# Attention and two expert layers on one core: copies, masks and minus maxima written by ScalarE, maxima over two PSUM banks, a predicated mean of v

## The chip, the cores and the metric

The kernel runs on one core of a Trainium2 chip. The metric is the device time of one execution in microseconds (us). Before the change three runs took 762.19, 762.69 and 763.52 us; the median is 762.69 us.

## The reference

For 2 batches of 8 heads, 768 rows and 64 columns a clustered attention is computed; its output goes through a dense layer and then through a layer of 8 experts. The change touches only the attention:

```python
q_assign = np.argmax(np.einsum('bhsd,hcd->bhsc', q_n, c_n), axis=-1)   # 16 clusters
k_assign = np.argmax(np.einsum('bhsd,hcd->bhsc', k_n, c_n), axis=-1)
mask = q_assign[:, :, :, None] == k_assign[:, :, None, :]
scores = scale * np.matmul(q, k.transpose(0, 1, 3, 2))
scores = np.where(mask, scores, -1000000000.0)
scores = scores - np.max(scores, axis=-1, keepdims=True)
attn = np.exp(scores)
attn = attn / (np.sum(attn, axis=-1, keepdims=True) + 1e-09)
return np.matmul(attn, v)
```

A row of q whose cluster holds no key has only masked scores, all alike, so its output is the mean of v.

## The kernel before, in words

A head has 6 blocks of 128 rows of q and of k (`NC` = 6) and is worked on in two halves of 3 blocks (`HC` = 3), called units. 16 heads make 32 units, 16 for each batch. The numbers are fp32, held as an f16 part and an f16 remainder, so that TensorE works in f16.

- `load` brings k, q and v of a head by DMA; `prep1` writes the f16 parts and remainders of k and q into `pk1` (a ScalarE copy, a GpSimd subtraction) and sends `pk1` through a transposing DMA on SP's queue into `tk1` (head 0: through TensorE).
- `prep2` finds the clusters. TensorE multiplies with the centroids (`sim`), VectorE makes the one-hot matrix `oh` (maximum, comparison, tie-break with the weights `wt_c`). It then builds `pk2`, four blocks of 6 x 128 columns: 64 columns of q or k parts, 16 columns of one-hot mask times 32768 (`BIGM`), and a column that later takes the minus maximum. Before the change VectorE writes all of these; it also counts the keys of each cluster (`cnt`, through TensorE) and zeroes the q rows of an empty cluster (`alm`, `alb`), so that all their scores come out alike. `pk2` is transposed into `tk2`.
- `unit_max` computes the masked scores of a unit on TensorE (`sm`, 6 tiles of 128x384), takes each tile's row maxima on VectorE (L255), and writes minus the maximum into `pk2` (L260); a small transposing DMA makes `qb`.
- `unit` computes the scores again as `st` (two matmuls for each of 6 blocks of keys), ScalarE takes the exponential into `p32` and, but for three blocks in the first batch, into the f16 `ph`; GpSimd forms the remainder `pl`. TensorE multiplies with v into `pv` (`weigh`, held back by 3 blocks); VectorE divides (`den`, `rec`, `x3`); ScalarE and GpSimd write `xp`.

While unit i runs, `unit_max` of head i+1, `prep2` of head i+2 and `prep1` of head i+3 are emitted between its steps. A scheduler then orders each engine's instructions; every engine executes its list in order. Beside the attention of the first batch the weights of the dense layer are converted from 64-bit floats, in 16 chunks for `w_in` and 16 for `w_out` (`f64_chunk`: ScalarE, three VectorE operations L333, L334, L337, ScalarE, GpSimd). Beside the attention of the second batch the dense layer of the first batch runs (`moe1`, L442 and L456). The dense layer of the second batch and the experts follow after the attention.

Of the kernel before, what the change touches and what calls it, by code (L numbers as in the profile page):

```python
# [7 lines left out]
F32 = mybir.dt.float32  # L8
# [12 lines left out]
SX = 16.0  # L21
# [22 lines left out]
def tile_kernel(ctx: ExitStack, tc, q, k, v, centroids, w_in, w_out, s, b, w_gate, w1, w2, out, dbg=None):  # L44
# [28 lines left out]
    mm = ctx.enter_context(tc.tile_pool(name="mm", bufs=2, space=PSUM))  # L73
# [7 lines left out]
    tpa = a0.enter_context(tc.tile_pool(name="tpa", bufs=4))  # L81
    at = ExitStack()
# [13 lines left out]
    sm_p = right("sm_p", 2, space=PSUM)  # L96
# [36 lines left out]
    def prep1(i):  # L133
# [33 lines left out]
    _, wt_c = iota([P, C], [[-1, C]], C, 0, "wt_c")  # L167
# [20 lines left out]
    def prep2(i):  # L188
        bb, hh = heads[i]
        h = hd[i]  # L190
        pk1, tk1 = h.pop("pk1"), h["tk1"]
# [11 lines left out]
        oh = tmp.tile([P, 2 * NC, C], F32, name="oh")  # L203
# [13 lines left out]
        yield
        ohq = tmp.tile([P, NC, C], F32, name="ohq")
        nc.vector.scalar_tensor_tensor(out=ohq, in0=cnt.unsqueeze(1).broadcast_to([P, NC, C]), scalar=0.0,
                                       in1=oh[:, NC:2 * NC], op0=ALU.is_gt, op1=ALU.mult)  # L220
        al = small.tile([P, NC], F32, name="al")
        nc.vector.tensor_reduce(out=al, in_=ohq, axis=AX.X, op=ALU.add)
        alm = small.tile([P, NC], I32, name="alm")
        nc.vector.tensor_scalar(out=alm, in0=al, scalar1=-1.0, scalar2=None, op0=ALU.mult)
        alb = small.tile([P, NC], F32, name="alb")
        nc.vector.tensor_scalar(out=alb, in0=al, scalar1=BIGM, scalar2=None, op0=ALU.mult)
        yield
        nc.vector.scalar_tensor_tensor(out=pk2[:, 2, :, 64:64 + C], in0=ohq, scalar=BIGM,
                                       in1=alb.unsqueeze(2).broadcast_to([P, NC, C]), op0=ALU.mult, op1=ALU.subtract)
        nc.vector.tensor_copy(out=pk2[:, 3, :, 64:64 + C], in_=pk2[:, 2, :, 64:64 + C])  # L230
# [670 lines left out]
```

## Time and profile before

| | before |
|---|---|
| median of 3 runs | 762.69 us |
| profiled execution: its own time / span of its instructions | 762.88 us / 760.8 us |
| busy in the span: TensorE (PE), VectorE (DVE) | 651.7 us, 575.3 us |
| ScalarE (ACT), GpSimd (POOL) | 415.5 us, 292.8 us |
| mean granted TensorE clock | 0.959 |

The span runs from the first instruction to the last; 2.1 us lie around it. The sums over the span mix stages: an engine that is idle among the experts may be the full one in the attention. The stages are therefore read one by one.

### The profile page before, as it was taken

What the parts mean: (1) busy time and instruction counts of PE and PEld (TensorE: products, weight loads), DVE (VectorE), ACT (ScalarE), POOL (GpSimd) and SP (SyncE); (2) the same over time, 40 slices, a digit from 0 to 9 for tenths busy, and PEclk for the clock granted to TensorE, in tenths of its full rate; (3) what the DMA queues carried; (4) which work ended last, traced back from release to release, by engine and by line L of the source; (5) the groups of instructions that cost most, each with busy time, mean ns of one, the idle gap of its engine ahead of it and who ended that gap; (6) DMA issues with size and microseconds to landing.
All of it is one profiled execution on the core that took longest, in us unless ns stands there. A gap on an engine that the chain in (4) does not pass through costs nothing.

```text
span 760.8 us, 16129 instructions
## 1 busy us (share of the span) xinstructions
PE 651.7 (86%) x6171; PEld 422.8 (56%) x6171; DVE 575.3 (76%) x1271; ACT 415.5 (55%) x789; POOL 292.8 (38%) x335
## 2 busy tenths in 40 slices
PE   1467876888787889999999999999999979998984
PEld 1245654666554535566565565465477747776652
DVE  8999998979899997789962263266955748877871
ACT  5356655645667655556655252045713665767751
POOL 6346755545765546546444120011012312221211
PEclk9999887989998989999999999999999998999998
DMA  8565766566374444244201500018754397688840
GB/s 228 138 146 143 173 149 146 131 149 126 72 169 143 108 124 74 70 87 78 42 6 36 112 29 1 1 43 291 270 201 98 117 254 241 169 269 264 266 140 23
DMA packets 134483, 101.28 MB, mean 133 GB/s; under 512 B 110332, under 2 KB 116476, under 8 KB 132096
## 3 DMA queue, kind: packets, MB, share of 16 engines
q1 hardware_dynamic: 124304, 68.58, 36.6%
q10 hardware_dynamic: 6576, 22.06, 8.9%
q0 software_dynamic: 3520, 9.54, 3.5%
q8 instruction: 51, 0.84, 0.5%
q14 instruction: 32, 0.26, 0.1%
HBM read 85.05 MB, written 7.39 MB: 121 GB/s over the span
## 4 chain that ended last, share of the span: by engine, by line
PE 35%; DVE 27%; issue 18%; DMA 13%; POOL 4%; ACT 1%; SPq 0%; POOLq 0%; DVEq 0%; ACTq 0%
PE py L456 15%; PE ps L442 10%; DVE mxt L255 6%; DMA tk<-pk 5%; DMA out<-o,oid 3%; PE pv L279 3%; POOL yg L643 3%; DVE l L334 2%; DMA raw<-in_moe_w_out 2%; DVE r L447 2%; DVE l L333 2%; DVE m L337 2%; PE sm L252 2%; POOL out L686 2%; PE st L287 2%
## 5 line engine op out<-in xcount | busy, mean ns | idle before, releaser
L300 POOL TENSOR_TENSOR pl<-p,ph 128x384 f16<-128x384 f32 x128 | 128.0, 1005 | 102.9 <-ACT ph L297 50.7
L442 PE MATMUL ps<-xt,wi 128*128 128x384 f16 x768 | 137.2, 330 | 0.0
L456 PE MATMUL py<-wo,g 128*128 128x512 f16 x576 | 134.9, 384 | 1.6 <-ACT r L445 1.6
L292 ACT ACTIVATE p<-st 128x384 f32<-128x384 f32 x192 | 93.6, 491 | 61.1 <-PE st L289 55.7
L255 DVE TENSOR_REDUCE mxt<-sm 128x1 f32<-128x384 f32 x192 | 102.2, 545 | 16.0 <-PE sm L252 15.6
L442 PEld LDWEIGHTS <-wi 128*128 128x128 f16 x768 | 74.7, 99 | 51.1 <-issue 4.9
L252 PE MATMUL sm<-tk 128*128 128x384 f16 x192 | 65.3, 362 | 37.4 <-DVE mxt L255 30.2
L456 PEld LDWEIGHTS <-g 128*128 128x128 f16 x576 | 55.6, 99 | 63.8 <-issue 4.7
L287 PE MATMUL st<-tk,tk 128*128 128x384 f16 x192 | 66.1, 344 | 7.9 <-ACT ph L297 5.8
L297 ACT ACTIVATE ph<-st 128x384 f16<-128x384 f32 x144 | 70.2, 488 | 0.0
L289 PE MATMUL st<-qb,tk 128*128 128x384 f16 x192 | 66.0, 347 | 2.8 <-DMA qb<-pk 2.7
L448 ACT ACTIVATE g<-r,b 128x384 f16<-128x384 f32 x64 | 39.4, 616 | 51.4 <-DVE r L447 51.4
L680 PEld LDWEIGHTS <-ht 128*128 128x128 f16 x384 | 37.4, 99 | 52.6 <-issue 10.0
L449 DVE SCALAR_TENSOR_TENSOR g<-r,b,g 128x384 f16<-128x384 f32 x64 | 46.1, 720 | 18.5 <-ACT g L448 18.5
L279 PEld LDWEIGHTS <-ph 128*128 128x128 f16 x864 | 45.7, 101 | 20.5 <-issue 5.7
L523 POOL DMA_INDIRECT yreg<-yp,posi x12 | 12.5, 1042 | 113.1 <-DVE posi L509 88.1
L279 PE MATMUL pv<-v,ph 128*128 128x65 f16 x864 | 52.9, 197 | 1.6 <-ACT ph L297 1.5
L666 PE MATMUL hps<-x2t,wa 128*128 128x128 f16 x768 | 46.8, 223 | 5.5 <-DVE ht L671 5.5
L606 DVE SCALAR_TENSOR_TENSOR wa<-stg,wa 128x1024 f16<-128x1024 f32 x40 | 46.7, 1219 | 5.8 <-ACT wa L605 5.7
L666 PEld LDWEIGHTS <-wa 128*128 128x128 f16 x768 | 45.4, 100 | 7.5 <-issue 5.7
L686 POOL DMA_INDIRECT out<-o,oid x16 | 21.5, 1342 | 72.9 <-ACT o L685 64.2
L447 DVE SCALAR_TENSOR_TENSOR r<-r,s 128x384 f32<-128x384 f32 x64 | 46.7, 730 | 2.0 <-ACT r L445 2.0
(219 smaller groups left out, 1269.0 us busy)
## 6 DMA issues: line engine op xcount, KB each, us to landing
stg<-in_moe_w SPq DMA_DIRECT2D x44, 1024.0 KB, 6.0
raw<-in_moe_w_out ACTq DMA_DIRECT2D x16, 512.0 KB
stg<-in_moe_w ACTq DMA_DIRECT2D x8, 1024.0 KB, 7.6
raw<-in_moe_w_in ACTq DMA_DIRECT2D x10, 512.0 KB, 4.4
kqv<-in_k SPq DMA_DIRECT2D x16, 192.0 KB, 3.8
kqv<-in_q SPq DMA_DIRECT2D x16, 192.0 KB, 4.9
kqv<-in_v SPq DMA_DIRECT2D x16, 192.0 KB, 5.7
raw<-in_moe_w_in SPq DMA_DIRECT2D x6, 512.0 KB, 5.4
```

The source lines that it names most:

```text
L252: nc.tensor.matmul(out=sm, lhsT=tk2[:, 2, c0 + c, :], rhs=tk2[:, 0, n * HC:(n + 1) * HC, :].rearrange("p c x -> p (c x)"), start=True, sto ...
L255: nc.vector.tensor_reduce(out=mxt[:, c, n:n + 1], in_=sm, axis=AX.X, op=ALU.max)
L279: nc.tensor.matmul(out=pv[:, c, :], lhsT=p[:, c * P:(c + 1) * P], rhs=w, start=first[0], stop=(kc == NC - 1 and c == HC - 1 and p is parts ...
L287: nc.tensor.matmul(out=st, lhsT=tk1[:, 0, kc, :], rhs=tk2[:, 1, c0:c0 + HC, :].rearrange("p c x -> p (c x)"), start=True, stop=False)
L289: nc.tensor.matmul(out=st, lhsT=tk2[:, 0, kc, :], rhs=qb.rearrange("p c x -> p (c x)"), start=False, stop=True)
L292: nc.scalar.activation(out=p32, in_=st, func=AF.Exp, scale=1.0 / 8.0)
L297: nc.scalar.activation(out=ph, in_=st, func=AF.Exp, scale=1.0 / 8.0)
L300: eng.tensor_tensor(out=pl, in0=p32, in1=ph, op=ALU.subtract)
L442: nc.tensor.matmul(out=ps, lhsT=wi[:, a, kk, f * P:(f + 1) * P], rhs=xt[:, c, kk], start=(kk == 0 and n == 0), stop=(kk == KD - 1 and n == 2))
L447: nc.vector.scalar_tensor_tensor(out=g0, in0=r, scalar=s4, in1=r, op0=ALU.mult, op1=ALU.mult)
L456: st8["py"] = nc.tensor.matmul(out=ps, lhsT=g[:, a, f, c * P:(c + 1) * P], rhs=wo[:, w, f], start=(f == 0 and n == 0), stop=(f == KF - 1 a ...
L666: nc.tensor.matmul(out=ps[:, j], lhsT=ws[:, w, kk * F + f0:kk * F + f0 + P], rhs=xt[:, a, kk], start=(i == 0), stop=(i == 3 * KD - 1))
```

## The change

1. `pk1` gets a third block: ScalarE writes q's f16 part twice side by side straight from the loaded q (new L144). The first score matmul of `st` takes its moving operand from `tk1` instead of `tk2`. So the transposing DMA of `pk1` carries 18 blocks of 128 columns instead of 12, and that of `pk2` 12 instead of 18.
2. `pk2` has three blocks. ScalarE copies the parts into it (new L202, L203), multiplies the one-hot matrix (now f16) into the mask columns (new L223, L224) and writes the minus maxima (new L260). The VectorE operations for these are gone, and the count of keys, `ohq`, `al`, `alm` and `alb` too.
3. In place of the count, TensorE sums v over all keys (`vsp`, 12 matmuls), ScalarE scales it to the mean `vm` and makes a `flag` from the maxima (it is not zero where only masked scores were found); VectorE copies `vm` over `x3` where the flag says so (`copy_predicated`, new L317), once in each unit.
4. In the first batch (and head 8) `sm` is a tile of two PSUM banks, and one VectorE reduction takes the maxima of both. Four banks (`smw`, 2 buffers) serve this; the pools `mm` and `sm_p` open only after the first batch. So `pv` of the first batch has one bank, where it had one for each half of a head.
5. Head 0's transposes on TensorE write f16 into PSUM.

```diff
+        pk1 = pk.tile([P, 3, NC, P], F16, name="pk1")
+        nc.scalar.copy(out=pk1[:, 2].rearrange("p c (t d) -> p c t d", t=2),
+                       in_=kq[:, NC:2 * NC].unsqueeze(2).broadcast_to([P, NC, 2, D]))
...
+        nc.scalar.copy(out=pk2[:, 0, :, 0:D], in_=pk1[:, 0, :, 0:D])
+        nc.scalar.copy(out=pk2[:, 1:3, :, 0:D], in_=pk1[:, 1].rearrange("p c (t d) -> p t c d", t=2))
...
+        st8[f"a{i}"] = nc.vector.tensor_tensor(out=oh, in0=oh, in1=pm.unsqueeze(2).broadcast_to([P, 2 * NC, C]), op=ALU.is_equal)
+        nc.scalar.activation(out=pk2[:, 0, :, 64:64 + C], in_=oh[:, 0:NC], func=AF.Copy, scale=BIGM)
+        st8[f"b{i}"] = nc.scalar.activation(out=pk2[:, 1:3, :, 64:64 + C], func=AF.Copy, scale=BIGM, bias=-BIGM,
+                                            in_=oh[:, NC:2 * NC].unsqueeze(1).broadcast_to([P, 2, NC, C]))
...
+                nc.tensor.matmul(out=vsp, lhsT=ones16, rhs=v1[:, c, t, 1:1 + D], start=(c == 0 and t == 0), stop=(c == NC - 1 and t == 1))
+        nc.scalar.activation(out=vm, in_=vsp, func=AF.Copy, scale=SX / S)
-            nc.tensor.matmul(out=cnt, lhsT=ones16, rhs=pk2[:, 0, c, 64:64 + C], start=(c == 0), stop=(c == NC - 1))
...
-        nc.vector.tensor_tensor(out=pk2.bitcast(I32)[:, 2:4, :, 0:D // 2],
-                                in0=pk1.bitcast(I32)[:, 1].rearrange("p c (t d) -> p t c d", t=2),
-                                in1=alm.unsqueeze(1).unsqueeze(3).broadcast_to([P, 2, NC, D // 2]),
-                                op=ALU.bitwise_and)
...
...
+            sm = smw.tile([P, 2, 512], F32, name="sm") if i <= H else None
+                    nc.vector.tensor_reduce(out=mm1[:, c:c + 1], in_=sm[:, :, 0:HT], axis=AX.XY, op=ALU.max)
+        st8[f"c{i}{qh}"] = nc.scalar.activation(out=pk2[:, 2, c0:c0 + HC, 64 + C], in_=mm1, func=AF.Copy, scale=-1.0 / BIGM)
+        nc.scalar.activation(out=flag, in_=mm1, func=AF.Relu, scale=-1.0, bias=nokey)
...
-        pv = (mm.tile([P, HC, D + 1], F32, name="pv", tag="mm") if i < H and qh else pv_p.tile([P, HC, D + 1], F32, name="pv"))
+        pv = pv_p.tile([P, HC, D + 1], F32, name="pv")
...
-                             rhs=tk2[:, 1, c0:c0 + HC, :].rearrange("p c x -> p (c x)"), start=True, stop=False)
+                             rhs=tk1[:, 2, c0:c0 + HC, :].rearrange("p c x -> p (c x)"), start=True, stop=False)
...
+        nc.vector.copy_predicated(out=x3, mask=h["flag"][qh].bitcast(I32).unsqueeze(2).broadcast_to([P, HC, D]),
+                                  data=h["vm"].unsqueeze(1).broadcast_to([P, HC, D]))
```

**ScalarE at the start.** The list of ScalarE before the change, from the first copy into `pk1` to the first two copies of head 0's transposed parts (`tk1`, which the clusters wait for):

```order
L139 CAST pk1_168<-kqv_115 128x12x64
L147 CAST v1_192<-kqv_115 128x6x64
L153 COPY vw_197<-kqv_115 128x6x64
L361 ACT_TABLE_LOAD
L361 ACTIVATE r0_136<-n2_134 128x1
L139 CAST pk1_327<-kqv_287 128x12x64
L147 CAST v1_332<-kqv_287 128x6x64
L153 COPY vw_337<-kqv_287 128x6x64
L331 ACTIVATE m64_445<-raw_443 128x512
L123 CAST tk1_171<-st_172 128x384
```

The same place now, from the first copy of v on:

```order
L152 CAST v1_204<-kqv_112 128x6x64
L158 COPY vw_209<-kqv_112 128x6x64
L202 COPY pk2_0_128<-pk1_169 128x6x64
L142 CAST pk1_321<-kqv_287 128x12x64
L144 CAST pk1_321<-kqv_287 128x768
L152 CAST v1_327<-kqv_287 128x6x64
L158 COPY vw_332<-kqv_287 128x6x64
L203 COPY pk2_0_128<-pk1_169 128x12x64
L335 ACTIVATE m64_433<-raw_431 128x512
L202 COPY pk2_1_129<-pk1_321 128x6x64
L127 COPY tk1_173<-st_174 128x384
```

Five more copies (two L144, of heads 0 and 1, the first of them just above these rows, two L202 and one L203) stand ahead of the first copy into `tk1`.

**TensorE at the change of units.** TensorE before the change where the second half of head 2 begins its product with v (`pv_1302`; LDWEIGHTS belongs to the matmul below it):

```order
L252 MATMUL sm_1338<-tk2_1019 128x384
L252 LDWEIGHTS tk2_1019
L252 MATMUL sm_1346<-tk2_1019 128x384
L287 LDWEIGHTS tk1_429
L287 MATMUL st_1341<-tk2_724,tk1_429 128x384
L289 LDWEIGHTS tk2_724
L289 MATMUL st_1341<-qb_1104,tk2_724 128x384
L279 MATMUL pv_1302<-vw_436,p32_1306 128x65 x3
L252 LDWEIGHTS tk2_1019
L252 MATMUL sm_1361<-tk2_1019 128x384
L287 LDWEIGHTS tk1_429
L287 MATMUL st_1349<-tk2_724,tk1_429 128x384
```

The same unit now (`pv_1265`; `st_1320` and `st_1336` are its last two scores, `st_1390` the first of head 3):

```order
L291 MATMUL st_1320<-qb_1069,tk2_631 128x384
L289 LDWEIGHTS tk1_417
L289 MATMUL st_1336<-tk1_417 128x384
L291 LDWEIGHTS tk2_631
L291 MATMUL st_1336<-qb_1069,tk2_631 128x384
L289 LDWEIGHTS tk1_710
L289 MATMUL st_1390<-tk1_710 128x384
L291 LDWEIGHTS tk2_915
L291 MATMUL st_1390<-qb_1218,tk2_915 128x384
L281 MATMUL pv_1265<-vw_424,p32_1269 128x65 x3
L281 LDWEIGHTS ph_1293
L281 MATMUL pv_1265<-v1_419,ph_1293 128x65
```

Before, the product began when three of the unit's six scores had been issued, and went on between them. Now it begins behind all six and the first of the next unit, and its 36 matmuls stand in one piece, behind a wait for VectorE's reading of the one bank.

**VectorE between a product and its division.** Before the change, from `den` to `x3` of the first half of head 0:

```order
L308 TENSOR_SCALAR den_704<-pv_549 128x3
L255 TENSOR_REDUCE mxt_718<-sm_788 128x1
L333 TENSOR_SCALAR l64_2632<-raw_2628 128x512
L212 TENSOR_SCALAR pk2_3_130<-oh_893 128x6x16
L255 TENSOR_REDUCE mxt_718<-sm_803 128x1
L311 RECIPROCAL rec_706<-den_704 128x3
L334 SCALAR_TENSOR_TENSOR l64_2632<-m64_2630,l64_2632 128x512
L255 TENSOR_REDUCE mxt_850<-sm_918 128x1
L255 TENSOR_REDUCE mxt_850<-sm_851 128x1
L259 TENSOR_REDUCE mm1_806<-mxt_718 128x3
L313 TENSOR_TENSOR x3_708<-pv_549,rec_706 128x192
```

Now, from `den` of the first half of head 1 to its predicated copy:

```order
L310 TENSOR_SCALAR den_972<-pv_821 128x3
L338 SCALAR_TENSOR_TENSOR l64_2563<-m64_2561,l64_2563 128x512
L216 TENSOR_TENSOR oh_1154<-sim_1116,mx_1152 128x192
L313 RECIPROCAL rec_974<-den_972 128x3
L341 SCALAR_TENSOR_TENSOR m64_2561<-raw_2559,l64_2563 128x512
L218 TENSOR_TENSOR oh_1154<-oh_1154,wt_c_120 128x192
L315 TENSOR_TENSOR x3_976<-pv_821,rec_974 128x192
L337 TENSOR_SCALAR l64_2573<-raw_2569 128x512
L220 TENSOR_REDUCE pm_1164<-oh_1154 128x12
L317 COPY_PREDICATED x3_976<-flag_648,vm_411 128x192
```

Other work still stands between `den` and `x3`; fewer rows of it are maxima, and the bank is free when `x3` has been computed.

## Rows read from the trace of the kernel before

**Rows 1.** Windows by stage: length, busy us (x instructions) of each engine, clock, DMA

```profile
core 0: us, PE busy (x) PEld busy (x) DVE busy (x) ACT busy (x) POOL busy (x), PEclk, DMA share, GB/s
0.00:72.70 72.70, 35.00 (x367) 23.70 (x368) 69.20 (x168) 37.62 (x74) 38.48 (x69) 1.00 0.65 170
72.70:202.60 129.90, 102.98 (x1067) 77.43 (x1067) 118.36 (x295) 78.22 (x179) 77.46 (x88) 0.88 0.61 136
202.60:294.50 91.90, 76.92 (x639) 44.20 (x639) 87.69 (x160) 58.43 (x127) 53.66 (x50) 0.91 0.46 117
294.50:430.40 135.90, 130.39 (x1337) 79.49 (x1336) 92.77 (x257) 76.16 (x182) 64.46 (x81) 1.00 0.32 63
```

**Rows 2.** Timeline of ScalarE, the writes of xp: ends of heads 0, 7 and 15

```profile
72.33 0.35 ACT L316 CAST xp<-x 128x192 f16<-128x192 f32 x1 [1.94 <-DVE x L313]
...
202.29 0.35 ACT L316 CAST xp<-x 128x192 f16<-128x192 f32 x1 [0.50 <-DVE x L313]
...
430.02 0.35 ACT L316 CAST xp<-x 128x192 f16<-128x192 f32 x1
```

**Rows 3.** Groups by line and form, VectorE, whole span: busy us, mean ns

```profile
L260 DVE TENSOR_SCALAR pk<-mm 128x3 f16<-128x3 f32 x32 | 13.9, 435 | 0.2
L231 DVE TENSOR_TENSOR pk<-pk,alm 128x384 int32<-128x384 int32 x16 | 13.9, 869 | 0.0
L236 DVE COPY pk<-pk 128x768 f16<-128x768 f16 x16 | 13.8, 860 | 0.0
...
L230 DVE COPY pk<-pk 128x96 f16<-128x96 f16 x16 | 8.7, 542 | 0.5 <-DMA qb<-pk 0.5
...
L228 DVE SCALAR_TENSOR_TENSOR pk<-ohq,alb 128x96 f16<-128x96 f32 x16 | 7.8, 487 | 0.0
L224 DVE TENSOR_SCALAR alm<-al 128x6 int32<-128x6 f32 x16 | 7.3, 459 | 0.1
L238 DVE COPY pk<-pk 128x384 f16<-128x384 f16 x16 | 7.2, 448 | 5.2 <-DMA tk<-pk 3.5 <-ACT pk L139 1.7
L212 DVE TENSOR_SCALAR pk<-oh 128x96 f16<-128x96 f32 x16 | 6.4, 398 | 0.1
```

**Rows 4.** Single lines, whole span: ns min/median/max, first and last start

```profile
L236 DVE COPY pk<-pk x16: 341/922/1794, 23.9 to 368.8; 128x768 f16<-128x768 f16 x16
L231 DVE TENSOR_TENSOR pk<-pk,alm x16: 542/558/1506, 22.0 to 367.0; 128x384 int32<-128x384 int32 x16
L230 DVE COPY pk<-pk x16: 171/178/1624, 25.7 to 369.4; 128x96 f16<-128x96 f16 x16
L260 DVE TENSOR_SCALAR pk<-mm x32: 155/171/1400, 38.0 to 399.5; 128x3 f16<-128x3 f32 x32
L139 ACT CAST pk<-kqv x16: 815/832/847, 5.3 to 311.5; 128x768 f16<-128x768 f32 x16
```

**Rows 5.** Groups by line and form, ScalarE, whole span: busy us, mean ns

```profile
L316 ACT CAST xp<-x 128x192 f16<-128x192 f32 x32 | 11.3, 353 | 14.6 <-DVE x L313 14.4
L147 ACT CAST v<-kqv 128x384 f16<-128x384 f32 x16 | 8.4, 523 | 7.4 <-DMA kqv<-in_v 4.3 <-PE pv L279 3.1
...
L361 ACT ACTIVATE r<-n 128x1 f32<-128x1 f32 x1 | 0.2, 203 | 0.0
```

**Rows 6.** Timeline of VectorE, two maxima in a row; then a group, whole span

```profile
46.42 1.02 DVE L255 TENSOR_REDUCE mxt<-sm 128x1 f32<-128x384 f32 x2
...
L255 DVE TENSOR_REDUCE mxt<-sm 128x1 f32<-128x384 f32 x192 | 102.2, 545 | 16.0 <-PE sm L252 15.6
L206 DVE TENSOR_TENSOR oh<-oh,wt_c 128x192 f32<-128x192 f32 x16 | 8.0, 500 | 0.1
```

**Rows 7.** Groups by line and form, TensorE, whole span: busy us, mean ns

```profile
L279 PE MATMUL pv<-v,ph 128*128 128x65 f16 x864 | 52.9, 197 | 1.6 <-ACT ph L297 1.5
L279 PE MATMUL pv<-vw,p 128*128 128x65 f32 x288 | 45.1, 298 | 0.5 <-DVE x L313 0.4
...
L216 PE MATMUL cnt<-pk,ones 128*128 128x16 f16 x96 | 5.3, 173 | 9.4 <-DVE pk L212 9.4
```

**Rows 8.** Timeline of VectorE: den and x3 of one unit

```profile
108.55 0.15 DVE L308 TENSOR_SCALAR den<-pv 128x3 f32<-128x3 f32 x1
...
112.57 0.34 DVE L313 TENSOR_TENSOR x<-pv,rec 128x192 f32<-128x192 f32 x1
```

More of the change, by code (lines that the diff above doesn't have):

```diff
@@ L81, in tile_kernel @@
     tpa = a0.enter_context(tc.tile_pool(name="tpa", bufs=4))
+    smw = a0.enter_context(tc.tile_pool(name="smw", bufs=2, space=PSUM))
     at = ExitStack()
@@ L117, in transpose @@
         for g in range(0, src.shape[1], HC):
-            pool, name = ((st_p, "st"), (sm_p, "sm"))[g // HC % 2] if pools is None else pools
-            ps = pool.tile([P, HT], F32, name=name)
             nn = min(HC, src.shape[1] - g)
+            odd = g // HC % 2
+            if pool is not None:
+                ps = pool.tile([P, HC, P], F16, name="ct", tag="aux")
+            elif odd:
+                ps = smw.tile([P, 2, 8, P], F16, name="sm")[:, 0]
+            else:
+                ps = st_p.tile([P, HC, P], F16, name="st")
             for n in range(nn):
-                nc.tensor.matmul(out=ps[:, n * P:(n + 1) * P], lhsT=src[:, g + n], rhs=ident, start=True, stop=True)
-            (nc.scalar.copy if g // HC % 2 == 0 else nc.vector.tensor_copy)(
-                out=dst[:, g:g + nn], in_=ps[:, 0:nn * P].rearrange("p (n x) -> p n x", n=nn))
+                nc.tensor.transpose(out=ps[:, n], in_=src[:, g + n], identity=ident)
+            (nc.vector.tensor_copy if odd else nc.scalar.copy)(out=dst[:, g:g + nn], in_=ps[:, 0:nn])
     def load(i):
@@ L165, in iota @@
         return ti, tf
-    _, wt_c = iota([P, C], [[-1, C]], C, 0, "wt_c")
+    _, wt32 = iota([P, C], [[-1, C]], C, 0, "wt32")
+    wt_c = const.tile([P, C], F16, name="wt_c")
+    nc.vector.tensor_copy(out=wt_c, in_=wt32)
+    nokey = const.tile([P, 1], F32, name="nokey")
+    nc.gpsimd.memset(nokey, -BIGM * BIGM / 2)
     ones16 = const.tile([P, P], F16, name="ones16")
@@ L190, in prep2 @@
         h = hd[i]
-        pk1, tk1 = h.pop("pk1"), h["tk1"]
+        pk1, tk1, v1 = h.pop("pk1"), h["tk1"], h["v1"]
+        pk2 = pk2_of(i)
+        nc.scalar.copy(out=pk2[:, 0, :, 0:D], in_=pk1[:, 0, :, 0:D])
+        nc.scalar.copy(out=pk2[:, 1:3, :, 0:D], in_=pk1[:, 1].rearrange("p c (t d) -> p t c d", t=2))
         sim = aux.tile([P, 2 * NC, C], F32, name="sim", tag="aux")
@@ L206, in prep2 @@
         nc.vector.tensor_tensor(out=oh, in0=oh, in1=wt_c.unsqueeze(1).broadcast_to([P, 2 * NC, C]), op=ALU.mult)
-        pm = small.tile([P, 2 * NC], F32, name="pm")
+        pm = small.tile([P, 2 * NC], F16, name="pm")
         nc.vector.tensor_reduce(out=pm, in_=oh, axis=AX.X, op=ALU.max)
         yield
-        nc.vector.tensor_tensor(out=oh, in0=oh, in1=pm.unsqueeze(2).broadcast_to([P, 2 * NC, C]), op=ALU.is_equal)
-        pk2 = pk2_of(i)
-        st8[f"a{i}"] = nc.vector.tensor_scalar(out=pk2[:, 0, :, 64:64 + C], in0=oh[:, 0:NC], scalar1=BIGM, scalar2=None, op0=ALU.mult)
@@ L214, in prep2 @@
-        cnt = aux.tile([P, C], F32, name="cnt", tag="aux")
-        for c in range(NC):
-            nc.tensor.matmul(out=cnt, lhsT=ones16, rhs=pk2[:, 0, c, 64:64 + C], start=(c == 0), stop=(c == NC - 1))
[L217 to L229, printed above, removed]
@@ new lines, in prep2 @@
+        st8[f"b{i}"] = nc.scalar.activation(out=pk2[:, 1:3, :, 64:64 + C], func=AF.Copy, scale=BIGM, bias=-BIGM,
+                                            in_=oh[:, NC:2 * NC].unsqueeze(1).broadcast_to([P, 2, NC, C]))
+        yield
+        tk2 = tpool(i).tile([P, 2, NC, P], F16, name="tk2", bufs=4 if i < H else 2)
+        transpose(i, tk2.rearrange("p a c x -> p (a c) x"), pk2[:, 0:2].rearrange("p a c x -> p (a c) x"))
+        yield
+        vsp = aux.tile([P, D], F32, name="vsp", tag="aux")
@@ L243, in unit_max @@
+        for c in range(NC):
+            for t in range(2):
+                nc.tensor.matmul(out=vsp, lhsT=ones16, rhs=v1[:, c, t, 1:1 + D], start=(c == 0 and t == 0), stop=(c == NC - 1 and t == 1))
+        vm = tmp.tile([P, D], F32, name="vm", bufs=3)
+        nc.scalar.activation(out=vm, in_=vsp, func=AF.Copy, scale=SX / S)
+        h.update(pk2=pk2, tk2=tk2, qb={}, vm=vm, flag={})
     def unit_max(i, qh):
@@ L575, in tile_kernel @@
             a0.close()
+            mm = ctx.enter_context(tc.tile_pool(name="mm", bufs=2, space=PSUM))
+            sm_p = right("sm_p", 2, space=PSUM)
             wop = ctx.enter_context(tc.tile_pool(name="wop", bufs=1, reuse_waits="tile"))
```

45 lines of the change are left out of this document (18 added, 27 removed).

## The prediction

> **What bounds the kernel now.** I read the windows by stage first, cut at the ends of heads 0, 7 and 15 [rows 1, 2]. Up to the end of head 0 VectorE is busy 69.2 of 72.7 us: apart from the first microseconds it never rests. From there to the end of head 7 it is busy 118.4 of 129.9 us, TensorE 103.0, ScalarE 78.2, GpSimd 77.5. These are 7 heads, so a head takes 18.6 us, of which VectorE works 16.9, TensorE 14.7 (at a mean granted clock of 0.88), ScalarE 11.2, GpSimd 11.1. VectorE is the full engine here. In the first part of the second batch it is again VectorE (87.7 of 91.9 us); in the last part TensorE is full (130.4 of 135.9 us), and VectorE has room. After 430.4 us no instruction of the change runs. So time can be won up to 294.5 us, where VectorE sets it, and hardly later.
>
> Then the groups of the operations that go. Their means are far from what they need: the copy of 128x768 took 0.341 us at best, 0.922 in the median and 1.794 at worst, a copy of 128x96 between 0.171 and 1.624, while ScalarE's copy of 128x768 stays between 0.815 and 0.847 [rows 4]. VectorE pays for waits inside these instructions.
>
> **The change, part by part.** The sum is made against the profiled execution (762.88 us, 760.8 of span), 0.2 us above the median of the runs.
>
> *VectorE, removed.* The eight groups shown add up to 79.0 us over 16 heads, 4.94 us a head [rows 3]; three small ones (`ohq`, `al`, `alb`) are not counted. Two maxima of 0.545 us follow each other in 1.02, so neighbours overlap by about 0.07 us [rows 6]; nine instructions a head give back 4.94 - 0.63 = 4.3 us.
>
> *VectorE, two banks.* One maximum over 768 elements in place of two over 384. No row shows it. It costs at least one of 0.545 and at most both, 1.02 [rows 6]. A PSUM operation on 192 elements takes 0.34 [rows 8], so 192 more cost about 0.2 and 384 more about 0.4: I take 0.95, a saving of 0.07 a pair, 0.4 us a head.
>
> *VectorE, added.* The predicated copy of 128x192 is not in the trace. From below stands the 0.34 of `x3` [rows 8], from above the 0.87 of the operation on 128x384 with two operands in SBUF (L231) [rows 3]. Nearest is L206, the same size with two operands in SBUF: 0.50 [rows 6]. Less the overlap that is 0.43, twice a head, 0.86. Over 16 heads the ends make it 9 or 26 us; even the upper end leaves most of the saving.
>
> Net, VectorE loses 4.3 + 0.4 - 0.86 = 3.8 us a head in the first batch.
>
> *ScalarE, added.* Two copies of 128x768 by L139's 0.83, one of 128x384 by L147's 0.52, one of 128x192 by L316's 0.35, one of 128x96 between L361's 0.20 and L316's 0.35 (taken 0.28), `vm` 0.21, and four of 128x3 by L361's 0.20: 3.84 us a head [rows 4, 5].
>
> *TensorE.* 6 matmuls of `cnt` go (0.055 us each, 0.33), 12 of `vsp` come; they lie between `cnt` and the 0.061 of the product with v, of nearly their width [rows 7]: 0.66 to 0.73. So +0.4 us a head. It is free while TensorE waits, and costs 0.4 a head where it is full.
>
> *DMA transposes.* 30 blocks of 128 columns a head before and after; six of them move from `tk2`, which the maxima soon want, to `tk1`, which is written heads earlier. I cost it at nothing: the lead of `tk1` covers it, and in the first heads, where that lead is short, it is inside the range.
>
> *Stage by stage.* Up to head 0's end three preparations are in the window (L231 starts there three times), 12.9 us, about 1 from the maxima, less 0.9 for two predicated copies: 13 us of VectorE's work, all on the path. Against it, ScalarE gets 3.84 us for each of three heads there, some 12, and five copies (3.5 us) stand ahead of the first `tk1` copy in its list, which the clusters of head 0 wait for. I take a gain of **10**, between 4 and 13.
>
> Heads 1 to 7: eight preparations fall in the window, 34.4, plus 2.8, less 6.0: VectorE's 118.4 become 87.2, 12.5 a head. ScalarE gets 78.2 + 26.9 = 105.1, **15.0** a head, TensorE 105.8, **15.1**. The bound goes over from one engine to two that hand each other their results. Before, the full engine filled 91% of the time. At 91% a head would take 16.6 us, at 82% nothing would be won; I choose 88%, a little below what one engine reached, because two must now meet: 17.15 us a head, 1.4 less, **10** for seven heads, between 1 and 18.
>
> To 294.5 us: two preparations, 8.6, less 1.7: 6.9 of VectorE's 87.7. TensorE has 15 us of rest there. **5**, between 0 and 7. To 430.4 us: TensorE rests 5.5 us in all and gets some more work: **2**, between -2 and 4.
>
> 10 + 10 + 5 + 2 = 27 us: 762.9 - 27 = 735.9, less the 0.2 above the median, **735.7**.
>
> **A rule and the rows.** The trace shows the waits inside VectorE's copies, and none in ScalarE's [rows 4]. The Trainium skill, SBUF — State Buffer, section "Who interferes with whom", gives the reason: VectorE and GpSimd share a second port pair of SBUF as an exclusive lock, copies, `tensor_scalar` and operations with two SBUF inputs take it, and the loser waits for the whole instruction; ScalarE has ports of its own. By that rule the predicated copy, with mask and data in SBUF, waits too, as L206 does by its row. It also warns that a removed copy need not take its wait with it, since GpSimd works on and the next VectorE instruction may meet it. The sum goes by the means; the other reading is the second rival.
>
> **The rivals.**
>
> *More than that* (16%). The clock of 0.88 among heads 1 to 7 comes with TensorE's gaps. If it rises as the gaps close, TensorE's 15.1 fall to some 13.5, ScalarE alone is full, and at 94% a head takes 16.0: 18 us there. With the upper ends elsewhere 13 + 18 + 7 + 4 = 42: 720.7. Against it: the gaps do not close where ScalarE sets the pace.
>
> *The waits stay* (18%). If the removed operations give back only their best durations, the four of rows 4 save 1.36 instead of 3.14 a head, 1.78 less: VectorE loses 2.0 a head and stands at 14.9, beside 15.0 and 15.1. Three engines equally full fill 82% at best, and heads 1 to 7 win nothing; 5 at the start and 4 later remain: 753.7. For it: GpSimd's work does not shrink. Against it: an instruction that is gone cannot wait, and fewer of VectorE's can be hit.
>
> *The single bank* (12%, slower). A unit's product with v now waits until VectorE has read the bank of the unit before. That product is 27 f16 matmuls of 0.061 and 9 fp32 ones of 0.157 [rows 7], 3.1 us; `den` to the end of `x3` took 4.4 [rows 8]. Behind the waiting product stand the next scores in TensorE's list, so ScalarE runs out of scores. If ScalarE stands through the 3.1 and 1 of the 4.4, a unit takes its 7.5 of ScalarE's work and 4.1, 11.6 instead of 9.3: 14 units lose 32, the other stages win 17, the kernel ends at +15, 778. It decides from 10.5 us a unit on. Against it: the scores of the next unit stand ahead of the product in places (the change's lists show one), VectorE has fewer rows between `den` and `x3`, and the second batch has always had one bank.
>
> *Nothing moves* (4%): the gains are eaten by waits of ScalarE's list, in which copies that wait for GpSimd or VectorE now stand ahead of exponentials.
>
> **How the numbers follow.** The forecast holds 50%, with a range of its own of 726 to 746. Faster by over 0.2% (1.5 us, about what a measurement of this kernel can tell): 50 + 16 + 18 = 84%; within it 4%; slower 12%. The range of 718 to 758 takes in the rival of the waits and most of the one above, and leaves out the single bank and the far ends.
>
> **What would show it.** In the trace of the changed kernel: head 0 ends near 62 us and head 7 near 182; VectorE is below 75% busy between them and ScalarE above 80%; VectorE's whole busy time falls from 575 to about 510 us, ScalarE's rises from 416 to about 477; the predicated copies take 0.35 to 0.9 us each; from the end of head 15 on the length is unchanged. Wrong would be: `pv` matmuls that wait long for `x3` (the single bank), a predicated copy above 1 us, or remaining VectorE operations whose means rise toward those of the removed ones (the waits stay).

## The result, and the profile after

The changed kernel takes 769.89 us (median of 6 runs, 767.0 to 772.8) against 761.82 us: ratio 1.0134, 95% interval 1.0098 to 1.0171. It is slower by some 8 us; the forecast was 735.7. The profiled execution took 772.8 us, its span 771.1. A few executions ran slower than the others of their kernel; the medians below leave them out, and e17, whose profiled execution was one of them, gives no lengths.

The windows of the changed kernel, cut where [rows 1] are cut:

```profile
core 0: us, PE busy (x) PEld busy (x) DVE busy (x) ACT busy (x) POOL busy (x), PEclk, DMA share, GB/s
0.00:72.70 72.70, 44.98 (x417) 31.08 (x418) 61.84 (x120) 53.74 (x121) 41.96 (x73) 0.95 0.74 185
72.70:202.60 129.90, 102.34 (x1082) 76.01 (x1078) 84.24 (x165) 93.36 (x238) 72.28 (x84) 0.88 0.60 129
202.60:294.50 91.90, 75.78 (x666) 44.86 (x667) 83.58 (x137) 64.90 (x147) 55.36 (x52) 0.93 0.48 122
294.50:430.40 135.90, 129.66 (x1291) 78.44 (x1290) 85.95 (x223) 78.36 (x203) 56.17 (x73) 0.99 0.29 53
```

And the ends of heads 0, 7 and 15 in ScalarE's timeline, which answer to [rows 2]:

```profile
69.81 0.36 ACT L320 CAST xp<-x 128x192 f16<-128x192 f32 x1
...
201.12 0.37 ACT L320 CAST xp<-x 128x192 f16<-128x192 f32 x1
...
440.77 0.35 ACT L320 CAST xp<-x 128x192 f16<-128x192 f32 x1 [3.89 <-DVE x L317]
```

VectorE's work in the window of heads 1 to 7 fell from 118.4 to 84.2 us (86.2 between the changed kernel's own ends of heads 0 and 7), and the stretch did not get shorter: 131.3 us, before 130.0. The start won 2.5 us. From head 7 to head 15 the kernel lost 12 us (239.7, before 227.7). Behind head 15 nothing moved (330.3 us, before 330.8).

What TensorE waited for between 72 and 202 us (in all, times, longest):

```profile
PE sm L249 <- DMA tk<-pk: 9.3, 5, 3.0
PE pv L281 <- DVE x L315: 6.7, 6, 1.9
PE st L289 <- ACT ph L299: 4.8, 8, 1.0
```

And before:

```profile
PE sm L252 <- DVE mxt L255: 14.5, 12, 2.9
...
PE pv L279 <- DVE x L313: 0.4, 1, 0.4
```

The wait for the maxima has gone, the wait of the product with v for `x3` has come. One such wait in the timeline of all engines:

```profile
99.59 0.14 DVE L310 TENSOR_SCALAR den<-pv 128x3 f32<-128x3 f32 x1
...
102.20 0.16 DVE L313 RECIPROCAL rec<-den 128x3 f32<-128x3 f32 x1
102.27 0.32 PE L291 MATMUL st<-qb,tk 128*128 128x384 f16 x1
...
103.99 0.34 DVE L315 TENSOR_TENSOR x<-pv,rec 128x192 f32<-128x192 f32 x1
...
104.48 0.85 PE L281 MATMUL pv<-vw,p 128*128 128x65 f32 x6 [1.89 <-DVE x L315]
...
105.54 1.52 PE L281 MATMUL pv<-vw,p 128*128 128x65 f32 x6
...
109.03 0.36 PE L281 MATMUL pv<-v,pl 128*128 128x65 f16 x3
109.19 0.51 PE L289 MATMUL st<-tk 128*128 128x384 f16 x1
```

From `den` to `x3` VectorE takes 4.7 us, with other work between. TensorE stands for 1.89, then does the unit's product in one lump until 109.2; six fp32 matmuls soon take 1.52 us there instead of 0.85, as at the lower of the two clock levels (1.2 GHz; the granted clock is 0.66 between 100 and 120 us). The wait seen is 1.9 us, but from 102.59 to 109.19 no scores are made for ScalarE.

### The profile page after: what moved, and what is told of

Same layout as the page of the kernel before. It is cut to its first block, busy times and chain, and to the rows that moved or that the text cites. A ratio compares the mean times of both kernels' runs of the same rounds, so it can differ in the third digit from the quotient of the medians.

```text
span 771.1 us, 16233 instructions
## 1 busy us (share of the span) xinstructions
PE 663.4 (86%) x6267; PEld 430.8 (56%) x6267; DVE 529.0 (69%) x1040; ACT 461.7 (60%) x949; POOL 288.9 (37%) x336
## 4 chain that ended last, share of the span: by engine, by line
PE 39%; issue 17%; DVE 9%; DMA 9%; POOL 5%; ACT 2%; POOLq 0%; DVEq 0%; ACTq 0%
PE py L460 15%; PE ps L446 13%; DMA out<-o,oid 4%; PE pv L281 3%; DMA tk<-pk 3%; POOL yg L649 3%; DMA xt<-xp 2%; POOL out L692 2%; PE sm L249 2%; PE st L289 1%; PE hps L672 1%; PE st L291 1%; DVE mxt L253 1%; DVE r L451 1%; DVE l L338 1%
## 5 line engine op out<-in xcount | busy, mean ns | idle before, releaser
L302 POOL TENSOR_TENSOR pl<-p,ph 128x384 f16<-128x384 f32 x128 | 125.7, 989 | 131.4 <-ACT ph L299 69.0
L446 PE MATMUL ps<-xt,wi 128*128 128x384 f16 x768 | 140.5, 341 | 5.9 <-DMA xt<-xp 4.2
L460 PE MATMUL py<-wo,g 128*128 128x512 f16 x576 | 130.7, 379 | 1.1 <-ACT r L449 1.1
L446 PEld LDWEIGHTS <-wi 128*128 128x128 f16 x768 | 76.8, 102 | 66.7 <-issue 22.5
L249 PE MATMUL sm<-tk 128*128 128x384 f16 x192 | 57.3, 366 | 23.7 <-DMA tk<-pk 10.8
L289 PE MATMUL st<-tk 128*128 128x384 f16 x192 | 66.5, 346 | 9.8 <-ACT ph L299 7.6
L255 DVE TENSOR_REDUCE mm<-sm 128x1 f32<-128x768 f32 x54 | 50.6, 947 | 19.4 <-PE sm L249 19.4
L253 DVE TENSOR_REDUCE mxt<-sm 128x1 f32<-128x384 f32 x84 | 45.1, 549 | 23.8 <-PE sm L249 23.5
L281 PE MATMUL pv<-vw,p 128*128 128x65 f32 x288 | 47.0, 306 | 8.5 <-DVE x L315 8.5
L676 ACT ACTIVATE ht<-hps 128x512 f16<-128x512 f32 x32 | 18.8, 595 | 55.4 <-PE hps L672 41.2
```

The costliest lines, as they stand in the source:

```text
L249: nc.tensor.matmul(out=out, lhsT=tk2[:, 1, c0 + c, :], rhs=tk2[:, 0, n * HC:(n + 1) * HC, :].rearrange("p c x -> p (c x)"), start=True, st ...
L253: nc.vector.tensor_reduce(out=mxt[:, c, n:n + 1], in_=out, axis=AX.X, op=ALU.max)
L281: nc.tensor.matmul(out=pv[:, c, :], lhsT=p[:, c * P:(c + 1) * P], rhs=w, start=first[0], stop=(kc == NC - 1 and c == HC - 1 and p is parts ...
L289: nc.tensor.matmul(out=st, lhsT=tk1[:, 0, kc, :], rhs=tk1[:, 2, c0:c0 + HC, :].rearrange("p c x -> p (c x)"), start=True, stop=False)
L302: eng.tensor_tensor(out=pl, in0=p32, in1=ph, op=ALU.subtract)
L446: nc.tensor.matmul(out=ps, lhsT=wi[:, a, kk, f * P:(f + 1) * P], rhs=xt[:, c, kk], start=(kk == 0 and n == 0), stop=(kk == KD - 1 and n == 2))
```

## The experiments

Theory A: the single pv bank costs what the removed work wins. Theory B: the removed work lay beside a chain of latencies, and the bank costs little. Theory C: the last units have too little dense-layer work around them. The table gives, from the timelines of the profiled executions, the lengths of heads 1 to 7 and 8 to 15 (from one write of `xp` to the other) and the first matmul of the second batch's dense layer. Where an instruction moves, the order of others can move with it.

Each length is that of one execution, and it is not exact: up to the end of head 7 before and e4 have the same instructions in the same order on TensorE, VectorE, ScalarE and GpSimd, and their heads 1 to 7 differ by 6.3 us. For the changed kernel and e3 the same holds, and they differ by 0.0. The medians stand on 6 to 12 executions each.

| kernel | median us | ratio to before (95%) | heads 1–7 | heads 8–15 | dense layer 2 at |
|---|---|---|---|---|---|
| before | 760.2 to 761.8 | | 130.0 | 227.7 | 433.2 |
| changed | 769.9 | 1.0134 (1.0098–1.0171) | 131.3 | 239.7 | 441.1 |
| e1 two pv banks | 756.3 | 0.9944 (0.9907–0.9982) | 122.5 | 227.0 | 425.1 |
| e2 before, banks alone | 778.4 | 1.0235 (1.0195–1.0276) | 141.4 | 235.8 | 447.5 |
| e3 changed, 44 pieces | 772.4 | 1.0160 (1.0114–1.0207) | 131.3 | 236.2 | 435.6 |
| e4 before, 44 pieces | 759.4 | 0.9995 (0.9965–1.0024) | 123.7 | 229.9 | 427.4 |
| e5 e1, no mean of v | 748.6 | 0.9836 (0.9800–0.9872) | 119.2 | 227.8 | 420.0 |
| e6 e1, copies and masks back | 747.8 | 0.9843 (0.9809–0.9877) | 119.4 | 231.5 | 417.4 |
| e7 e1, one pv bank | 769.6 | 1.0115 (1.0071–1.0159) | 132.8 | 226.1 | 430.7 |
| e8 changed, pv bank from aux | 769.6 | 1.0137 (1.0097–1.0176) | 128.3 | 237.7 | 436.0 |
| e9 e1, copies back | 756.6 | 0.9955 (0.9923–0.9987) | 117.2 | 239.7 | 428.8 |
| e10 e1, no predicated copy | 753.1 | 0.9916 (0.9887–0.9945) | 125.4 | 231.0 | 424.7 |
| e11 e1, all four back | 759.5 | 0.9994 (0.9961–1.0027) | 115.0 | 238.0 | 429.9 |
| e12 e1, masks back | 749.8 | 0.9869 (0.9826–0.9911) | 114.7 | 235.4 | 415.8 |
| e13 changed, masks back | 765.2 | 1.0067 (1.0038–1.0096) | 129.2 | 229.7 | 430.6 |
| e14 e12, masks on both engines | 759.1 | 0.9975 (0.9941–1.0009) | 127.4 | 230.4 | 426.4 |
| e15 e1, masks swapped | 754.6 | 0.9919 (0.9884–0.9954) | 123.5 | 237.2 | 426.1 |
| e16 changed, masks swapped | 776.0 | 1.0197 (1.0141–1.0254) | 131.5 | 239.7 | 441.4 |
| e17 e1, 44 pieces | 764.7 | 1.0049 (1.0015–1.0083) | | | |

**e1** puts the PSUM layout of before under the changed kernel. The cut shows its two main places; one reduction for each bank, and the pools `mm` and `sm_p` open from the start, come with them:

```diff
-                out = sm[:, n, 0:HT] if i <= H else sm_p.tile([P, HT], F32, name="sm")
+                out = (mm.tile([P, HT], F32, name="sm", tag="mm") if n and c == 1 and i < H else
+                       sm_p.tile([P, HT], F32, name="sm"))
...
-        pv = pv_p.tile([P, HC, D + 1], F32, name="pv")
+        pv = (mm.tile([P, HC, D + 1], F32, name="pv", tag="mm") if i < H and qh else pv_p.tile([P, HC, D + 1], F32, name="pv"))
```

> The changed kernel with the PSUM layout of before: single-bank maxima, pv in two banks in the first batch. Theory A (the single pv bank eats the gain of heads 1 to 7): TensorE no longer waits for x3 (6.7 us between 72 and 202 us), head 7 ends at 185 to 194 us instead of 201.1, the total is 758 to 764 us. Theory B (the removed VectorE work lay beside a chain of latencies, and the bank costs little): head 7 ends within 3 us of 201, VectorE is busier by some 3 us over the heads for the extra maxima, and the total stays at 767 to 773 us. Theory C (the last heads run out of dense-layer work for TensorE to fill with): whatever head 7 does, TensorE is idle for 4 us or more in the last 35 us before the dense layer of batch 1 starts, and the total is no better than that of before.

**e2** is the reverse: these edits alone in the kernel before.

> The kernel before with one edit alone: maxima over two banks and one pv bank in the first batch. Theory A: TensorE waits for x3 of the unit before, 5 us or more between heads 1 and 7, head 7 ends 5 to 12 us later than 202.3, total 767 to 775 us. Theory B: head 7 ends within 3 us of 202.3, since the maximum over two banks saves as much as the bank costs; total 760 to 766 us. Theory C has no part in the first batch; if the end of head 15 is bare too, the total is up to 8 us over that of before.

e1 took 756.3 us, 13.6 below the changed kernel and 0.6% below before; e2 lost 2.35%. Both fell on theory A's side, and the totals by more than written (e1's head 7 ended at 196.0, 2 us late of its bounds, e2's 12.3 us after that of before). In e2 TensorE waited only 3.5 us for `x3`, where 5 or more were written. TensorE's waits of e1 in the same stretch have no `x3` left:

```profile
PE sm L250 <- DVE mxt L253: 9.6, 10, 2.7
PE pv L278 <- POOL pl L299: 3.5, 3, 2.6
PE sm L250 <- DMA tk<-pk: 3.3, 4, 1.1
```

In e2 the group of fp32 products shows the wait and the lower clock (0.82 between 72.7 and 202.6 us): a mean of 338 ns, where e1 has 292.

```profile
L287 PE MATMUL pv<-vw,p 128*128 128x65 f32 x228 | 42.9, 338 | 3.5 <-DVE x L321 3.5
```

**e3, e4** change `STEPS` to (5, 5, 5, 5, 6, 6, 6, 6), in the changed kernel and in before.

> The changed kernel with 44 instead of 52 pieces of the first batch's dense layer given out after heads 8 to 15 (STEPS 5,5,5,5,6,6,6,6), so that 12 instead of 4 are left behind the last head. Theory C: the dense layer's matmuls cover the last units, TensorE's idle time in the last 35 us before the dense layer of batch 1 falls from 5.7 us to under 2, the total falls by 4 to 8 us to 762 to 766. Theories A and B: the units of heads 8 to 15 were held by their own chain, the pieces only move behind it, and the total stays within 2 us of 769.9 or rises.

> The kernel before with the same STEPS (5,5,5,5,6,6,6,6). Theory C: the end of head 15 was covered already (TensorE 14.6 of the last 14.6 us), so no gain: within 2 us of 761.8. If it gains 4 us or more like the changed kernel, the number of pieces is a gain of its own that has nothing to do with the change.

In e3 TensorE's rest in the last 35 us fell from 5.95 to 3.14 us, not below 2, and the time did not fall. Theory C did not hold in this form. e4's heads 1 to 7 became 6.3 us shorter, though up to there nothing differs from before, neither the work nor its order. So much can lie between two executions:

```profile
72.33:202.29 129.96, 102.97 (x1067) 77.43 (x1067) 118.42 (x296) 78.28 (x178) 77.52 (x87) 0.88 0.61 136
```

```profile
72.25:195.93 123.68, 101.61 (x1067) 77.14 (x1067) 119.15 (x296) 78.44 (x179) 76.84 (x87) 0.89 0.65 144
```

The first row is of before, the second of e4, with columns as above.

**e7** is e1 with one pv bank, the maxima in single banks. It parts the two halves of the bank edit:

```diff
-        pv = (mm.tile([P, HC, D + 1], F32, name="pv", tag="mm") if i < H and qh else pv_p.tile([P, HC, D + 1], F32, name="pv"))
+        pv = pv_p.tile([P, HC, D + 1], F32, name="pv")
```

> The kernel with two pv banks, single-bank maxima kept, but every pv in the one bank of pv_p. Theory A (the pv bank alone): TensorE waits for x3, head 7 ends at 201 to 212 us instead of 196.0, total 766 to 778 us. Rival (it is the two-bank maxima: two long slots instead of three short ones, TensorE's maxima in lumps): head 7 within 2 us of 196.0, total 754 to 759 us.

It loses all of e1's gain and waits as the changed kernel does:

```profile
PE sm L250 <- DMA tk<-pk: 7.8, 4, 4.7
PE pv L278 <- DVE x L312: 7.4, 7, 3.3
```

ScalarE's wait for scores in the same stretch grows with it, from e1 (first row) to e7:

```profile
ACT p L291 <- PE st L288: 7.5, 13, 1.3
```

```profile
ACT p L291 <- PE st L288: 18.9, 19, 4.5
```

These 11.4 us more are near the 10.4 by which heads 1 to 7 grew. But e6, e9 and e10 wait 16 to 21 us for scores with two banks, so such a wait has other sources too. Of the 11.3 us between the spans of e1 and e7, 5.7 lie behind the start of the second dense layer, where both run the same number of matmuls; the start takes back 3.7.

**e8** has both, two-bank maxima and a second pv bank, by taking `aux` away in the first batch: `sim`, `vsp` and the centroids use slots of the maxima.

> The changed kernel with both: two-bank maxima in the first batch and a second pv bank, the bank taken from aux, whose three uses in the first batch (centroids, sim, vsp) take their turn in the two slots of the maxima. Theory A: head 0 ends at 69 to 71 us as in the changed kernel, head 7 at 188 to 197, total 748 to 757 us. Rival (the slots of the maxima are as scarce as the pv bank: sim holds one until VectorE's is_equal, the maxima wait for it): head 7 ends at 198 us or later, total over 760 us.

By its total the rival held (769.6; head 7 ended at 197.6, where it wrote 198 or later). Its mechanism shows little, 3.1 us of waits for the slots of the maxima. TensorE no longer waits for `x3`, but 12.1 us for `ph`; why ScalarE is late there is not shown. So a second pv bank taken from `aux` brought nothing back.

```profile
PE st L291 <- ACT ph L301: 12.1, 9, 2.6
PE sm L251 <- DVE mm L257: 3.1, 3, 1.6
```

**e5, e10** take parts of the mean of v out of e1: e5 all of it (`vsp`, `vm`, `flag`, the predicated copy), e10 the predicated copy.

> The kernel with two pv banks (run e1_two_pv_banks) without the mean of v: the vsp matmuls, vm, flag and the predicated copy are left out, so queries of empty clusters get no mean. If part 3 of the change is nearly free beside other work: 753 to 757 us, within 0.4% of that run's 756.3. If the predicated copy (0.5 us and more, behind the lock of the shared port) stands between x3 and the end of a unit on the path of all 32 units: 740 to 750 us.

> The kernel with two pv banks without the predicated copy alone (vsp, vm and flag stay; queries of empty clusters get no mean). If the predicated copy makes the 7.7 us that the mean costs: 747 to 751 us. If the 192 matmuls of vsp and ScalarE's vm and flag make them: 753 to 757 us. Between: both.

The mean costs 7.7 us, more than "nearly free" and at the edge of the other case. The copy alone gave 3.2, with intervals that overlap e1's; how the 7.7 divide stays open.

**e6, e9, e12, e11** put work of e1 back on VectorE: copies and masks, copies, masks, and all with minus maxima and flags. The masks' edit:

```diff
-        nc.scalar.activation(out=pk2[:, 0, :, 64:64 + C], in_=oh[:, 0:NC], func=AF.Copy, scale=BIGM)
+        nc.vector.tensor_scalar(out=pk2[:, 0, :, 64:64 + C], in0=oh[:, 0:NC], scalar1=BIGM, scalar2=None, op0=ALU.mult)
...
```

> The kernel with two pv banks with the copies of q and k and the two masks of prep2 written by VectorE again (only these; the rest as in that run). If the move to ScalarE is what gained the 6.3 us of heads 1 to 7: head 7 ends at 199 to 203 us instead of 196.0, total 759 to 763. If ScalarE's queue holds the masks up as much as VectorE did, or VectorE is not on the path of these heads: total within 2 us of 756.3 either way.

> The kernel with two pv banks, with only the two copies of q and k back on VectorE; the masks stay on ScalarE. If it is the copies, which stand on ScalarE ahead of exponentials and wait there for transposes that still read the packed tile (5.7 us in heads 1 to 7): 746 to 751 us, as with copies and masks back (747.8). If it is the masks, which wait on ScalarE for VectorE's one-hot: 754 to 758 us, as with none back (756.3).

> The kernel with two pv banks with the two masks alone back on VectorE; the copies of q and k stay on ScalarE. The copies alone back gave 756.6 us, both back 747.8, none 756.3. If the masks alone carry the gain of having both back: 746 to 750 us. If copies and masks must both leave ScalarE for the gain, or if the gain lies in where the other instructions come to stand when anything is moved: 753 to 759 us. In heads 1 to 7 the copies should tell: head 7 at 194 to 198 us, as with all on ScalarE (196.0), not at 188.5 to 190.7 as in the three runs with the copies back.

> The kernel with two pv banks with copies, masks, minus maxima and flags all on VectorE, so that of ScalarE's added work only the third block of the first packed tile and vm are left. If what stands on ScalarE's queue ahead of exponentials is the cost: 744 to 748 us, at or below the 747.8 of copies and masks back. If VectorE has become the bound again (15 us a head before): 749 to 754 us.

e6 and e12 win 8.5 and 6.5 us, e9 nothing. So the masks carry it; e6 missed both of its cases. But e12's head 7 ended at 184.8, not at 194 to 198: the copies on ScalarE do not keep heads 1 to 7 long. e11 missed: its heads 1 to 7 are as short as e12's, but it ends head 15 only 1.3 us before the kernel before (428.7), e12 9.8 (420.2). It has the masks on VectorE like e6, and takes 11.7 us more.

**e14** leaves the masks on VectorE, and ScalarE writes them once more, for nobody; **e15** swaps the two masks of e1; **e13** gives the changed kernel e12's edit.

```diff
+        mk = tmp.tile([P, 3, NC, C], F16, name="mk")
+        nc.scalar.activation(out=mk[:, 0], in_=oh[:, 0:NC], func=AF.Copy, scale=BIGM)
...
```

> The kernel with the two masks back on VectorE (749.8 us), in which ScalarE writes the same masks a second time to a tile that nobody reads. If ScalarE's 0.64 us a head for the masks, ahead of exponentials, is the cost: back to 754 to 759 us. If it is the hand-over from VectorE to ScalarE ahead of the transpose of the second packed tile: 748 to 752 us.

> The kernel with two pv banks (756.3 us) with its two masks on ScalarE written in the opposite order, the work being the same. If the time is set by the work and its engines: 754 to 758 us. If several us hang on the order into which the instructions fall: outside of that, 750 or 762 us.

> The changed kernel as it is (one pv bank, two-bank maxima) with the two masks alone back on VectorE. If masks and bank cost apart from each other: 769.9 less 6.5, 762 to 765 us. If the single bank holds these heads whatever ScalarE does: 768 to 772 us.

e14 lost 9.3 us: writing the masks costs on ScalarE though no transpose waits for them. Its two groups take 10.4 us over 16 heads, and 4.9 more in waiting for the one-hot:

```profile
L229 ACT ACTIVATE mk<-oh 128x192 f16<-128x192 f16 x16 | 5.8, 360 | 0.0
L228 ACT ACTIVATE mk<-oh 128x96 f16<-128x96 f16 x16 | 4.6, 288 | 4.9 <-DVE oh L223 4.9
```

e15 came out 1.7 us below e1, although TensorE's list, of the same 6267 matmuls, differs in 2166 places; its heads 8 to 15 are 10 us longer. e13 won 4.7 us: the masks cost beside one bank too, and the bank layout costs 15.4 without them (e13 against e12).

**e16** swaps the masks in the changed kernel, **e17** is e1 with e3's `STEPS`.

> The changed kernel (769.9 us) with the two masks on ScalarE written in the opposite order, the work being the same. If the 12 us between heads 7 and 15 belong to the change (late pools for the dense layer, two-bank maxima up to head 8): that stretch again takes 236 to 242 us, total 768 to 772. If they come from the order into which dense layer and last units fall: the stretch takes 227 to 233 us, total 760 to 766.

> The kernel with two pv banks (756.3 us) with 44 instead of 52 pieces of the first batch's dense layer given out after heads 8 to 15. The same number cost the changed kernel 2.5 us and won before 1.4, both within or near the intervals. If the number of pieces matters little: 753 to 759 us, the stretch between heads 7 and 15 at 225 to 232 us.

e16 repeats the 239.7 us of heads 8 to 15 and comes to 441.4 like the changed kernel. But the swap left the order as it was: TensorE's list is the same in all 6267 places, and apart from the exchanged masks VectorE's and ScalarE's lists differ in four places each, between 25 and 27 us. So e16 cannot part its two cases. Its span is 4.3 us longer, 4.0 of it behind that point, in the same instructions in the same order, and its median 6.1. A few us between two kernels can therefore mean nothing. e17 missed: fewer pieces cost e1 8.4 us.

## Why the prediction was wrong

The step that failed is in *Heads 1 to 7*: "The bound goes over from one engine to two that hand each other their results", with 17.15 us a head. It gave the single pv bank no term; the bank stood as a rival at 12%. The nine kernels with the change's other parts and the old layout (e1, e5, e6, e9 to e12, e14, e15) took 114.7 to 127.4 us for heads 1 to 7; the five with pv in one bank (changed, e3, e7, e13, e16) 129.2 to 132.8, and e2 141.4 against 130.0 and 123.7 for the list of before (before, e4). On the median the bank costs 13.3 to 17.7 us in four pairs (e1 and changed, e1 and e7, e12 and e13, before and e2). Only e1 and e7 differ in the pv bank alone (13.3 us, with intervals apart, and twice the 6.1 by which e16 stands above the changed kernel); in the other pairs the maxima and the opening of the pools change with it. With the layout of before the change comes to 756.3 us (e1), 0.6% below before. The mechanism is the rival's; its price of 32 us was too high, a unit took 9.4 us (131.3 / 14) instead of 11.6, against 8.7 in e1. It decided at less than the 10.5 us a unit given there, because the other stages did not win the 17 us set against it. "The second batch has always had one bank" was a weak argument against it: there TensorE's list has dense-layer matmuls between the units (read from the order, not tried).

The Trainium skill, PSUM — Partial Sum Buffer, section "Summary: rules for kernel authors", says that reading PSUM while matmuls run wants a different bank, with the guard set by bank. The trace agrees: 6.7 us of waits for `x3` with one bank, none with two in e1 and 0.4 before.

With two banks the step was near: heads 1 to 7 took 122.5 us, 7.5 less than before, where 10 were forecast; one execution is not sure enough to say how near.

The bank is not the whole miss. In the profiled executions the start fell 7.5 us short of the forecast, heads 1 to 7 fell 11.3 short, and heads 8 to 15 18.9.

*Start*: forecast 10, measured 2.5. "All on the path" was wrong. VectorE worked 61.8 instead of 69.2 us in that window (59.3 up to the changed kernel's own end of head 0), and other waits took over; TensorE's, up to 70 us:

```profile
PE sim L210 <- ACT vm L236: 5.0, 2, 3.0
PE sm L249 <- DVE mm L255: 3.8, 5, 1.3
PE vsp L234 <- DVE oh L216: 3.0, 2, 2.1
```

`vsp` and the next head's `sim` share the bank `aux`, so that `sim` waits until ScalarE has read `vsp`. No term had that. Before, `cnt` lay in the same bank, and VectorE read it.

*Heads 8 to 15*: forecast 7 won, measured 12 lost. The changed kernel's TensorE at the end of head 15:

```profile
436.13 0.35 PE L281 MATMUL pv<-v,ph 128*128 128x65 f16 x6
438.98 0.27 PE L281 MATMUL pv<-v,pl 128*128 128x65 f16 x3 [2.50 <-POOL pl L302]
439.09 0.35 PE L281 MATMUL pv<-v,ph 128*128 128x65 f16 x6
439.27 0.25 PE L281 MATMUL pv<-v,pl 128*128 128x65 f16 x3
441.08 2.40 PE L446 MATMUL ps<-xt,wi 128*128 128x384 f16 x7 [1.55 <-DMA xt<-xp]
```

And before, at the same place:

```profile
428.88 0.25 PE L279 MATMUL pv<-v,pl 128*128 128x65 f16 x3
428.96 0.29 PE L483 MATMUL lg<-wg,yt 128*128 128x8 f16 x6
429.12 4.26 PE L456 MATMUL py<-wo,g 128*128 128x512 f16 x19
433.21 0.65 PE L442 MATMUL ps<-xt,wi 128*128 128x384 f16 x3
```

Before, 19 matmuls of the first dense layer still lay behind the last unit; in the changed kernel they had come earlier, and the last unit and the transpose of `xp` stood bare. That makes 7.9 us at the first matmul of the second dense layer (441.08 - 433.21); the other 2.4 us between the spans lie behind it. From the end of head 7 to the end of head 15 TensorE worked 211.0 us, before 206.9, so that most of the 12 us, 7.8, is rest. Whether the change or the order brings this loss is not settled. The layout alone does not: e7 and e13 with one pv bank take 226.1 and 229.7 us there, e9 and e11 with two take 239.7 and 238.0, and fewer pieces (e3) did not cure it. That order can do as much is seen in e15, which does the work of e1 in another order and takes 10 us more there; but e15 is no slower in the end, so a longer stretch is not yet a loss of time.

*The single prices*, over the whole span:

```profile
L317 DVE COPY_PREDICATED x<-flag,vm x32: 360/384/1804, 59.9 to 440.4; 128x192 f32<-128x192 int32 x32
...
L255 DVE TENSOR_REDUCE mm<-sm x54: 920/947/958, 28.9 to 175.1; 128x1 f32<-128x768 f32 x54
```

The maximum over two banks took 0.947 us (0.95). The predicated copy took 0.680 in the mean (0.50), within its bounds, but six of the 32 took more than the 1 us that the prediction named as a sign of being wrong. 15 took 0.65 us or more; each of these began while an operation of GpSimd ran, and each ended 0.23 to 0.24 us behind the end of one. One of them:

```profile
105.39 1.27 POOL L344 TENSOR_TENSOR wi<-m,wi 128x512 f16<-128x512 f32 x1
...
105.57 1.32 DVE L317 COPY_PREDICATED x<-flag,vm 128x192 f32<-128x192 int32 x1
```

With this the trace agrees with the Trainium skill's rule of the shared port (SBUF — State Buffer, section "Who interferes with whom"). That a removed copy need not take its wait with it is the prediction's inference from that rule. In heads 1 to 7 the waits did not pass to what stayed: VectorE's 84.2 us between 72.7 and 202.6 are below the 87.2 of the sum, so that rival fell. Some operations that stayed did grow: the subtraction for the remainder of v took 957 ns, before 704.

Over the span VectorE went from 575.3 to 529.0 us, not to 510; the prediction's own terms (4.3 and 0.86 a head over 16 heads, 0.4 over 8) give 517. ScalarE went from 415.5 to 461.7 instead of 477. Its added operations sum to 65.6 us, but neighbours overlap there too, and the sum took that out for VectorE alone.

*ScalarE*, 3.84 us a head, was counted only as load. With two banks, 0.65 us a head less of it (the masks) was worth 6.5 us (e12) and beside the copies 8.8 (e6 against e9), with one bank 4.7 (e13), and putting them back for nobody cost 9.3 (e14); since a few us can mean nothing, the sign is well supported and the size is not. More work on VectorE is not better: e11 lost the gain again.

The best kernels that compute all of it, e6 (747.8 us) and e12 (749.8), keep the change's other savings, leave pv two banks and write the masks on VectorE: 1.6 and 1.3% below before.

## What to carry to other kernels

A PSUM bank that is given up is an edit with a price of its own: look for who reads it last and what the producer can do until then. A full engine that gets relieved gives time only if no other edit of the same change puts a wait in its place, so cost each edit by itself and try each by itself. Where two executions of one instruction list differ by 6 us in a stretch, and an edit can move the order besides, single comparisons of a few us prove little; put several kernels with and without the edit side by side. A test of order has to change the order: compare the lists before reading anything into the time.

## What was not expected of the hardware

The clock fell behind a stretch with short rests, the longest of them 1.89 us: between 100 and 105 us TensorE was busy 2.0 us, and between 107 and 110 us, fully busy, it had a granted clock of 0.50, the lower level (1.2 GHz). Six fp32 matmuls took 1.52 us there instead of 0.85. This is one place; no run parts the wait for `x3` from the rests before it.

The same instructions in the same order took 330.0 us (changed) and 334.1 us (e16) from the first matmul of the second dense layer to the end, in the profiled executions. Over all kernels but e17, with 2732 to 2765 matmuls left at that point, it was 326.3 us (e13) to 335.5 us (e3).
